# Where the key and value weights begin inside their rows: 64 or 0 bytes past a multiple of 256

## The chip, the core and the metric

The kernel runs on one core of one Trainium2 chip. The metric is the device time of one execution in microseconds (us). Before the change the median of three runs is 750.0 us (749.83 to 750.37).

The core has five engines that run side by side: TensorE (PE in the profile; its loads of stationary operands are listed apart as PEld), VectorE (DVE), ScalarE (ACT), GpSimd (POOL) and SyncE (SP), which here issues the DMAs. A matmul on TensorE has a stationary operand, loaded ahead of it, and a moving operand, streamed past it column by column from SBUF, the core's working memory. Its result lands in PSUM.

## The reference

The kernel mixes two blocks that read the same input x of 2048 tokens by 640 features, with a gate per token:

```python
g = sigmoid((x * gate_w).sum(-1, keepdims=True))
# a: linear attention, 32 heads of 20 features
q, k, v = split(x @ wqkv)
phi_q = concat([softmax(q @ w_phi), softmax(-(q @ w_phi))])   # per head
phi_k = concat([softmax(k @ w_phi), softmax(-(k @ w_phi))])
o = phi_q @ (phi_k.T @ v) / (phi_q @ phi_k.sum(tokens) + 1e-6)
a = o @ wo
# b: feed-forward of width 1728
b = silu(x @ w1) @ w2
return g * a + (1 - g) * b
```

All inputs and the output are float32.

## The kernel before, in words

Every product of float32 matrices is made from two parts of each operand: a high part, which is the value rounded to the matmul's own format, and a low part, the rest. Three products are summed (PASSES: high times high, high times low, low times high), so each matrix product has three passes over the five chunks of 128 input features, fifteen matmuls for one block of output columns.

The work has four stages.

1. **Keys and values.** The key weights are first multiplied with the feature map w_phi (`k_weights`, L332), so that keys come out mapped. Together with the value weights and the gate vector they form 1282 columns. They are kept in two SBUF tiles, `wh` (high parts) and `wl` (low parts), made by `big_kv`. Each holds five rows per partition, one for each chunk of input features, WS = 1344 float32 apart (5376 bytes, 21 times 256). A loop over 16 tiles of 128 tokens then multiplies: the stationary operand is a piece of x (`xa`, 128 by 128), the moving operand is a part of a row of `wh` or `wl`. The first two token tiles are worked while the weights still arrive (`kv_share`, L344), the other fourteen by `kv_proj` (L489). After the products of a tile, `kv_rest` (L470) and `kv_acc` (L459) add the outer products of mapped keys and values of a tile two turns earlier.
2. **Feed-forward**, blocks of 512 tokens: the hidden layer (L537, and L554 for its first four columns of tiles) and the output (L726), both with 512 moving columns.
3. **Queries**, 128 tokens at a time (L448, two halves of 320 columns).
4. **Numerators and output projection**, 256 tokens at a time (L1140 and L1182, 256 columns).

The order on TensorE, VectorE, ScalarE and GpSimd is the order in which the code is written; within the `inorder` blocks it is pinned. All DMAs are issued by SyncE.

The 1282 columns are cut into three parts, one for each PSUM bank: columns 0 to 480, 480 to 980 and 980 to 1282 (CUTS), hence 480, 500 and 302 columns wide. PLACE says at which float32 of a row each part begins: 16, 528 and 1040. The function `w_cols` turns a range of columns into its place in the row, and all who write or read the tiles use it: `k_split_w` and `v_weights`, which write the high part with ScalarE (L125) and the low part with VectorE (L127), and `kv_share` and `kv_proj`, whose matmuls stream it.

The two tiles begin at a multiple of 256 bytes in SBUF and their rows are a multiple of 256 bytes long, so all fifteen parts of a tile begin 64 bytes past a multiple of 256. The pieces of x, the weights and inputs of the feed-forward and of the queries begin at a multiple of 256. The output projection's weights begin 48 float32 (192 bytes) into their tile (WOFF), and the rows it streams at a multiple of 256.

Of the kernel before, what the change touches and what calls it, by code (L numbers as in the profile page):

```python
# [53 lines left out]
WC = 2 * D + 2  # L54
RAW = D + 16
CUTS = (0, 480, 980, WC)
PLACE = (16, 528, 1040)
WS = 1344
VC = PLACE[2] + CUTS[3] - CUTS[2] - (PLACE[1] + D - CUTS[1])
BIG = NC * WS  # L60
# [7 lines left out]
def mix_kernel(ctx: ExitStack, tc: tile.TileContext, xT, wqT, wkc, wkr, wv, bd, bdc, cst, wo, w1, w1r, w2, out):  # L68
# [212 lines left out]
    def part_of(lo, hi):  # L281
        return next(k for k in range(3) if CUTS[k] <= lo and hi <= CUTS[k + 1])

    def w_cols(lo, hi):

        k = part_of(lo, hi)
        return slice(PLACE[k] + lo - CUTS[k], PLACE[k] + hi - CUTS[k])

# [1100 lines left out]
```

## Time and profile before

| | |
|---|---|
| median of 3 runs | 750.0 us (749.83 to 750.37) |
| the profiled execution | 749.77 us |
| its span, first to last instruction | 747.9 us |
| TensorE busy | 742.9 us (99%), 4177 matmuls |
| VectorE, ScalarE, GpSimd busy | 347.5, 264.1, 255.3 us |
| DMA | 50.30 MB, 67 GB/s on average |

The profile is of one execution. It lists groups of instructions by source line (L489 is line 489 of the kernel), engine and operation, with the names of the tile written and of those read, the shape of the operands and a count. A matmul's listed duration reaches from its start to the end of its results, and the next one begins before that: matmuls overlap. What a matmul costs in a dense row of matmuls is the distance from its start to the next start, here called its pitch, which is read from start times in the timeline. Stationary loads (PEld) run beside the matmul before theirs.

### The profile page before, as it was taken

What the parts mean: (1) busy time and instruction counts of PE and PEld (TensorE: products, weight loads), DVE (VectorE), ACT (ScalarE), POOL (GpSimd) and SP (SyncE); (2) the same over time, 40 slices, a digit from 0 to 9 for tenths busy, and PEclk for the clock granted to TensorE, in tenths of its full rate; (3) what the DMA queues carried; (4) which work ended last, traced back from release to release, by engine and by line L of the source; (5) the groups of instructions that cost most, each with busy time, mean ns of one, the idle gap of its engine ahead of it and who ended that gap; (6) DMA issues with size and microseconds to landing.
All of it is one profiled execution on the core that took longest, in us unless ns stands there. A gap on an engine that the chain in (4) does not pass through costs nothing.

```text
span 747.9 us, 10458 instructions
## 1 busy us (share of the span) xinstructions
PE 742.9 (99%) x4177; PEld 648.8 (87%) x4177; DVE 347.5 (46%) x619; ACT 264.1 (35%) x477; POOL 255.3 (34%) x158
## 2 busy tenths in 40 slices
PE   9999999999999999999999999999999999999998
PEld 8899988888888888888888888888898899999988
DVE  5676666676751230112301122032566776867652
ACT  5444443346452321123111221123553534345230
POOL 2488777867200000000000000000174578686540
PEclk9999999999999999999999999999999999999999
DMA  8111111103660130001300013022102221221222
GB/s 264 50 54 53 54 54 53 60 15 103 199 206 1 34 121 1 1 0 40 119 0 1 0 41 122 35 77 65 47 29 99 79 98 58 85 78 57 71 87 78
DMA packets 35304, 50.30 MB, mean 67 GB/s; under 512 B 3546, under 2 KB 22890, under 8 KB 35255
## 3 DMA queue, kind: packets, MB, share of 16 engines
q1 hardware_dynamic: 35255, 49.63, 20.4%
q8 instruction: 33, 0.54, 0.3%
q14 instruction: 16, 0.13, 0.1%
HBM read 38.51 MB, written 11.11 MB: 66 GB/s over the span
## 4 chain that ended last, share of the span: by engine, by line
PE 98%; DMA 1%; SPq 0%; ACT 0%; DVE 0%; issue 0%
PE acc L726 25%; PE ph L537 23%; PE kvp L489 16%; PE pa L1182 10%; PE pq L448 10%; PE pn L1140 3%; PE pT L1007 2%; PE kv L459 2%; PE kvp L554 2%; PE kvp L344 1%; PE kvq L344 1%; PE pwq L239 1%; PE pwk L332 1%; DMA wvr<-wv 1%; PE kvp L470 0%; SPq L190 0%
## 5 line engine op out<-in xcount | busy, mean ns | idle before, releaser
L127 DVE TENSOR_TENSOR u<-ph,u 128x512 fp32r<-128x512 f32 x48 | 33.2, 692 | 186.2 <-ACT u L125 186.2
L726 PE MATMUL acc<-u,w 128*128 128x512 f32 x480 | 113.6, 391 | 0.0
L909 POOL MEMSET kvw<- 120x40 f32 x1 | 0.1, 131 | 309.8 <-PE ph L537 309.8
L726 PEld LDWEIGHTS acc<-u,w 128*128 128x128 f32 x480 | 89.7, 188 | 18.6
L537 PE MATMUL ph<-xf,w 128*128 128x512 f32 x420 | 99.3, 390 | 0.0
L540 ACT ACTIVATE ph<-ph 128x512 f32<-128x512 f32 x48 | 27.9, 582 | 190.4 <-PE ph L537 190.3
L489 PE MATMUL kvp<-wh,xa 128*128 128x480 f32 (+2 forms) x420 | 93.4, 359 | 0.0
L537 PEld LDWEIGHTS ph<-xf,w 128*128 128x128 f32 x420 | 78.7, 188 | 16.2
L489 PEld LDWEIGHTS kvp<-wh,xa 128*128 128x128 f32 x420 | 72.5, 189 | 8.6
L1182 PE MATMUL pa<-oT,wo 128*128 128x256 f32 x600 | 77.0, 282 | 0.0
L1182 PEld LDWEIGHTS pa<-oT,wo 128*128 128x128 f32 x600 | 73.8, 188 | 0.8 <-DVE oT L1161 0.8
L824 POOL TENSOR_TENSOR ez<-eq,zbc 128x1280 f32<-128x1280 f32 x16 | 47.0, 2938 | 79.9 <-ACT eq L807 55.9
L726 PE MATMUL acc<-u,f 128*128 128x512 f32 x300 | 71.6, 391 | 0.0
L537 PE MATMUL ph<-xf,f 128*128 128x512 f32 x300 | 71.3, 390 | 0.0
L537 PEld LDWEIGHTS ph<-xf,f 128*128 128x128 f32 x300 | 56.3, 188 | 11.7
L726 PEld LDWEIGHTS acc<-u,f 128*128 128x128 f32 x300 | 56.1, 188 | 11.5
L127 POOL TENSOR_TENSOR ph<-ek,ph 128x1280 fp32r<-128x1280 f32 x16 | 47.4, 2965 | 27.6 <-ACT ph L125 27.6
L448 PE MATMUL pq<-wq,xb 128*128 128x320 f32 x360 | 55.9, 313 | 0.0
L448 PEld LDWEIGHTS pq<-wq,xb 128*128 128x128 f32 x360 | 52.9, 188 | 2.0 <-DVE oT L1161 1.6
L489 PE MATMUL kvp<-wl,xa 128*128 128x480 f32 (+2 forms) x210 | 47.9, 359 | 0.0
L807 ACT ACTIVATE eq<-eq 128x1280 f32<-128x1280 f32 x16 | 20.4, 1276 | 66.4 <-DVE eq L439 66.4
L489 PEld LDWEIGHTS kvp<-wl,xa 128*128 128x128 f32 x210 | 37.0, 189 | 4.8
(158 smaller groups left out, 1058.9 us busy)
## 6 DMA issues: line engine op xcount, KB each, us to landing
wr<-w SPq DMA_DIRECT2D x26, 320.0 KB, 4.2
xrf<-xT SPq DMA_DIRECT2D x20, 256.0 KB, 3.6
fb_d<-o SPq DMA_DIRECT2D x20, 256.0 KB, 2.4
y<-fb_d SPq DMA_DIRECT2D x16, 256.0 KB, 2.8
out<-y SPq DMA_DIRECT2D x16, 256.0 KB, 2.2
xra<-xT SPq DMA_DIRECT2D x14, 256.0 KB, 3.0
xrb<-xT SPq DMA_DIRECT2D x12, 256.0 KB, 2.7
wvr<-wv SPq DMA_DIRECT2D x5, 327.0 KB, 5.2
```

Source lines behind the costliest of these rows:

```text
L127: eng.tensor_tensor(lo, src, hi.bitcast(F32), op=ALU.subtract)
L344: nc.tensor.matmul(kv_cols(t, lo, hi), x_of(t)[c][:, hx, :], WKV[hw][:, c, w_cols(lo, hi)], start=(opens and hx == 0 and hw == 0), stop=(c ...
L448: nc.tensor.matmul(dst, xt[c][:, hx, :], w[:, c, hw, lo : lo + n], start=first, stop=(hx == 1 and c == NC - 1))
L459: nc.tensor.matmul(kvt[i // 2][: KF + 1, i % 2, :, :KF], vs[t % VB][:, i, : KF + 1], ph[:, :, i * KF : (i + 1) * KF], start=(t == 0 and i ...
L489: nc.tensor.matmul(kv_cols(t, lo, hi), xt[c][:, hx, :], WKV[hw][:, c, w_cols(lo, hi)], start=(n == 0), stop=(n == 3 * NC - 1), skip_group_ ...
L537: nc.tensor.matmul(ph, lhs, rhs, start=(n == 0), stop=(n == len(todo) - 1))
L540: nc.scalar.activation(hs, ph, AF.Silu)
L726: nc.tensor.matmul(acc[m], lhs, rhs, start=(f == order[0] and n == 0), stop=(f == order[-1] and n == len(todo) - 1))
L807: nc.scalar.activation(Q[t]["e"], Q[t]["e"], AF.Exp)
L824: nc.gpsimd.tensor_tensor(ez, Q[t]["e"], zbc, op=ALU.mult)
L1140: nc.tensor.matmul(pns[u, gp][side * CT : side * CT + lhs.shape[-1], a, :], lhs, f[:w, k * 256 : (k + 1) * 256], start=True, stop=True,)
L1182: nc.tensor.matmul(pa[:, a, :], WO[:, c, hw, ds] if c < NG else WOR[:, ds], o[:, ho, c, :] if c < NG else o[:GW, ho, c, :], start=(k == 0) ...
```

## The change

The three parts of each row are moved 16 float32 (64 bytes) towards its beginning, so that they begin at a multiple of 256 bytes. Their widths, the distance between rows, the size of the tiles and the order of all instructions are as they were.

```diff
 CUTS = (0, 480, 980, WC)
-PLACE = (16, 528, 1040)
+PLACE = (0, 512, 1024)
 WS = 1344
 VC = PLACE[2] + CUTS[3] - CUTS[2] - (PLACE[1] + D - CUTS[1])
```

## The prediction

> **What bounds the kernel now.** I read the page's busy shares and its chain first, then TensorE's list of waits, then the groups of matmuls by form, and last the timeline of TensorE, because the question is what one matmul costs from start to next start.
>
> ```profile
> span 747.9 us, 10458 instructions
> PE 742.9 (99%) x4177; PEld 648.8 (87%) x4177; DVE 347.5 (46%) x619; ACT 264.1 (35%) x477; POOL 255.3 (34%) x158
> PEclk9999999999999999999999999999999999999999
> PE 98%; DMA 1%; SPq 0%; ACT 0%; DVE 0%; issue 0%
> PE acc L726 25%; PE ph L537 23%; PE kvp L489 16%; PE pa L1182 10%; PE pq L448 10%; PE pn L1140 3%; PE pT L1007 2%; PE kv L459 2%; PE kvp L554 2%; PE kvp L344 1%; PE kvq L344 1%; PE pwq L239 1%; PE pwk L332 1%; DMA wvr<-wv 1%; PE kvp L470 0%; SPq L190 0%
> ```
>
> ```profile
> PE warm L313 <- DVE ones L166: 1.0, 1, 1.0
> PE kvp L344 <- ACT wh L125: 0.4, 1, 0.4
> PE pT L1007 <- DVE oT L1163: 0.3, 1, 0.3
> ```
>
> TensorE is the whole path: 98% of the chain, at full granted clock in all slices, and idle for 1.7 us in three waits. The change touches the matmuls of lines L489 and L344, which hold 18% of that chain. With nothing waiting in front of them, a nanosecond more or less on each of these matmuls is a nanosecond of the span, so the whole forecast is a count of matmuls times a change in their pitch (start to next start).
>
> **The change, part by part.** No instruction is added, removed or moved in order. The width of the DMA'd value weights, VC, comes out at 654 columns both ways (1040+302-688 and 1024+302-672), so DMA sizes, packets and SyncE's queue stay as they are; the row width WS and the buffers stay too, so no other tile moves. Two things get another address: what ScalarE and VectorE write into the two weight tiles, and what TensorE streams out of them.
>
> The writes:
>
> ```profile
> L125 ACT CAST wh<-pwk x10: 292/425/558, 8.7 to 21.3; 128x480 fp32r<-128x480 f32 x5, 128x160 fp32r<-128x160 f32 x5
> L125 ACT CAST wh<-wvr x6: 439/738/742, 4.3 to 15.8; 128x654 fp32r<-128x654 f32 x4, 128x340 fp32r<-128x340 f32 x1, 128x302 fp32r<-128x302 f32 x1
> ```
>
> These are 16 writes by ScalarE (and 16 alike by VectorE) inside the first 22 us, beside the opening matmuls. What covers them is that TensorE waited for them only once, the 0.4 us above. If another address sped them up, at most that 0.4 us goes; if it slowed them a little, about as much comes. I take 0 and leave 0.4 us each way.
>
> The reads are the whole matter. How many there are:
>
> ```profile
> L489 PE MATMUL kvp<-wh,xa x420: 300/380/416, 32.1 to 172.3; 128*128 128x480 f32 x56, 128*128 128x500 f32 x42, 128*128 128x302 f32 x42
> L489 PE MATMUL kvp<-wl,xa x210: 302/382/396, 33.2 to 171.6; 128*128 128x480 f32 x35, 128*128 128x500 f32 x35, 128*128 128x302 f32 x35
> L344 PE MATMUL kvp<-wh,xa x34: 235/350/492, 5.0 to 24.7; 128*128 128x302 f32 x10, 128*128 128x480 f32 x10, 128*128 128x500 f32 x6, 128*128 128x340 f32 x4
> L344 PE MATMUL kvq<-wh,xa x34: 238/318/426, 5.2 to 32.0; 128*128 128x302 f32 x10, 128*128 128x480 f32 x10, 128*128 128x500 f32 x6, 128*128 128x340 f32 x4
> L344 PE MATMUL kvp<-wl,xa x17: 236/381/425, 5.6 to 24.1; 128*128 128x302 f32 x5, 128*128 128x480 f32 x5, 128*128 128x500 f32 x3, 128*128 128x340 f32 x2
> L344 PE MATMUL kvq<-wl,xa x17: 273/323/396, 5.8 to 31.8; 128*128 128x302 f32 x5, 128*128 128x480 f32 x5, 128*128 128x500 f32 x3, 128*128 128x340 f32 x2
> ```
>
> 420+210+34+34+17+17 = 732 matmuls. L489 runs 14 tokens' tiles times 15 for each of the three parts, 210 each; with L344's 30, 18 and 30 that makes 240 of 480 columns, 228 of 500, 240 of 302; the other 24 are parts of 340 and 160 columns.
>
> What one costs now, from the timeline of one token tile (first number the start in us, the count at the end of the line; a run that goes from the 480s to the 500s is merged, the line of 10):
>
> ```profile
> 102.25 1.26 PE L489 MATMUL kvp<-wh,xa 128*128 128x480 f32 x5
> 103.35 1.26 PE L489 MATMUL kvp<-wl,xa 128*128 128x480 f32 x5
> 104.44 2.40 PE L489 MATMUL kvp<-wh,xa 128*128 128x480 f32 x10
> 106.68 1.30 PE L489 MATMUL kvp<-wl,xa 128*128 128x500 f32 x5
> 107.82 1.30 PE L489 MATMUL kvp<-wh,xa 128*128 128x500 f32 x5
> 108.96 0.49 PE L459 MATMUL kv<-ph,v 128*121 128x240 f32 x3
> 109.29 0.86 PE L489 MATMUL kvp<-wh,xa 128*128 128x302 f32 x5
> 109.99 0.86 PE L489 MATMUL kvp<-wl,xa 128*128 128x302 f32 x5
> 110.69 0.86 PE L489 MATMUL kvp<-wh,xa 128*128 128x302 f32 x5
> 111.39 0.26 PE L470 MATMUL kvp<-ph,v 128*121 128x208 f32 x1
> ```
>
> 480 columns: (104.44-102.25)/10 = 219.0 ns. 500 columns: (108.96-106.68)/10 = 228.0 ns. 302 columns: (111.39-109.29)/15 = 140.0 ns. All three stream rows that begin 64 bytes past a multiple of 256, against stationary tiles (the x tiles) that begin at a multiple of 256.
>
> What matmuls cost whose streamed rows and stationary rows both begin at a multiple of 256, as all of these will after the change:
>
> ```profile
> 536.85 3.56 PE L726 MATMUL acc<-u,w 128*128 128x512 f32 x15
> 540.25 4.56 PE L448 MATMUL pq<-wq,xf 128*128 128x320 f32 x30
> 544.64 3.59 PE L537 MATMUL ph<-xf,w 128*128 128x512 f32 x15
> ```
>
> 512 columns: 3.40/15 = 226.7 ns. 320 columns: 4.39/30 = 146.3 ns. The line through the two is (226.7-146.3)/192 = 0.419 ns a column, and gives 213.3 ns at 480, 221.7 at 500, 138.8 at 302. The key and value matmuls now lie 5.7, 6.3 and 1.2 ns above it. **The end below:** if the shift puts them on the line, 240 x 5.7 + 228 x 6.3 + 240 x 1.2 = 3.1 us are saved.
>
> But two rows speak for the present offset. The output projection is the one other large group whose two operands begin 64 bytes apart modulo 256 (its stationary rows begin at WOFF, 192 bytes, its streamed rows at 0):
>
> ```profile
> 673.63 1.93 PE L1182 MATMUL pa<-oT,wo 128*128 128x256 f32 x15
> 675.40 0.29 PE L1182 MATMUL pa<-oT,wor_s 120*128 120x256 f32 x1
> ```
>
> 1.77/15 = 118.0 ns at 256 columns, where the line gives 119.5: this distance costs 1.5 ns less than none. And line L459 runs ten matmuls a tile in which the streamed rows step by 480 bytes and the stationary rows by 488, so that the distance between the two changes by 8 bytes from one to the next. Stationary rows are read one matmul ahead, so the fourth and the fifth are those that stream while the next weights are read at the same place modulo 256, or 8 bytes off it. Three looks into one tile's ten (ns, least/median/most):
>
> ```profile
> L459 PE MATMUL kv<-ph,v x3: 270/271/273, 58.8 to 59.0; 128*121 128x240 f32 x3
> L459 PE MATMUL kv<-ph,v x2: 271/274/278, 59.3 to 59.4; 128*121 128x240 f32 x2
> L459 PE MATMUL kv<-ph,v x2: 271/272/273, 59.4 to 59.5; 128*121 128x240 f32 x2
> ```
>
> The first look holds matmuls one to three, the second the fifth and sixth, the third the sixth and seventh: the fifth takes 278 ns, the others 270 to 273. So reading the stream and the next weights in step has cost 6 ns here. That the weights are indeed read beside the stream is in the loads' own row, 189 ns each, hidden in the pitches above:
>
> ```profile
> L489 PEld LDWEIGHTS kvp<-wh,xa 128*128 128x128 f32 x420 | 72.5, 189 | 8.6
> ```
>
> **The end above:** 732 x 6 = 4.4 us lost; with the output projection's 1.5 ns it would be 732 x 1.5 = 1.1 us. The change takes away exactly the distance that these rows reward, and the line that speaks the other way is drawn through whole multiples of 64 columns, which 480, 500 and 302 are not. I therefore take the side of the loss, and the mean of its two rows since they are equally near, 3.75 ns: 732 x 3.75 = 2.7 us.
>
> A rule of the Trainium skill stands against that. TensorE: Matmul & The Clock Gate (Part 2, step 1) says that TensorE has two independent read ports of SBUF, and that loading the next weights takes no read bandwidth from the running matmul. By that rule the address could not matter and the sum would be 0; the fifth matmul of L459 does not look like it, though nothing before the change isolates the address.
>
> **Sum.** The profiled execution took 749.77 us for a span of 747.9; with 2.7 us it becomes 750.6 and 752.5. The median of the runs is 750.0, 0.2 above it, so 752.7.
>
> **The rivals.** *First, the excess goes (faster).* The 5.7, 6.3 and 1.2 ns above the line come from streamed rows that begin off a multiple of 256, and vanish: 750.0-3.1 = 746.9 us. For it: 500 columns now cost 228.0 ns and 512 aligned ones 226.7, so something besides length is paid. Against it: 302 columns, at the same offset, pay only 1.2. It decides the sign as soon as the pitches at 480 and 500 fall by more than the 302s rise.
>
> *Second, the address does not matter (no change):* 750.0 us, within the 0.4 us of the writes. For it: the 320-column and 512-column groups cost what they cost with both operands at the same place and no waits, so being in step is harmless there. Against it: the excess at 480 and 500, and L459. This is what the skill's rule on two read ports, named above, would make of it. SBUF — State Buffer (Operand start alignment) asks only for starts at a multiple of the element size and says itself that this is about legality, not speed.
>
> *Third, last blocks are paid whole (slower still).* If an aligned row is read in whole pieces of 256 bytes, 480 and 500 columns cost as much as 512 and 302 as much as 320: 240 x (226.7-219.0) + 228 x (226.7-228.0) + 240 x (146.3-140.0) = 1.8-0.3+1.5 = 3.1 us, and with the 2.7 above 5.8: 755.8 us. For it: the aligned groups in this trace are only whole pieces and cannot deny it. Against it: 480 columns at the present offset also touch eight pieces and are 7.7 ns below 512.
>
> **How the numbers follow.** Forecast (loss of the distance, 752.7) 0.46; third rival 0.14; first 0.28; second 0.12. A measurement of this kernel tells about 0.2%, 1.5 us, from no change: slower is 0.46+0.14 = 0.60, same 0.12, faster 0.28. The range runs from the first rival to the third with the writes' 0.4 us at its ends, 746.8 to 756.2; beyond it I leave the larger losses and gains that no row bounds. The forecast's own range, from 1.5 and 6 ns each, is 751.1 to 754.4.
>
> **What would show it.** In the profile after, the timeline of a token tile: forecast, 480, 500 and 302 columns at about 223, 232 and 144 ns; first rival, 213, 222 and 139; second, 219, 228 and 140; third, 230, 230 and 150. The means of these forms among L489's groups must move by as many nanoseconds, the groups of L726, L537, L448 and L1182 must not move, and the stage of L489 must carry all of the difference. The prediction is wrong if 480 and 500 fall towards the line, or if another stage moves.

## The result, and the profile after

The changed kernel takes 747.93 us (median of 10 runs, 747.34 to 748.16) against 749.9 us before, a ratio of 0.9973 with a 95% interval of 0.9963 to 0.9982. It is 2.0 us faster; the forecast was 2.7 us slower.

The head of the page after, and the row of the L489 matmuls with the high parts (least, median and most duration in ns, then the first and the last start in us):

```profile
span 746.0 us, 10458 instructions
## 1 busy us (share of the span) xinstructions
PE 741.4 (99%) x4177; PEld 648.0 (87%) x4177; DVE 347.3 (47%) x619; ACT 264.1 (35%) x477; POOL 255.3 (34%) x158
```

```profile
L489 PE MATMUL kvp<-wh,xa x420: 297/378/396, 32.1 to 170.4; 128*128 128x480 f32 x56, 128*128 128x500 f32 x42, 128*128 128x302 f32 x42
```

The L489 matmuls start at 32.1 us in both kernels. The last starts at 170.4 in place of 172.3, so the stage is 138.3 us long in place of 140.2, and from there to the end it is 575.6 us both before (747.9-172.3) and after (746.0-170.4). The gain is in the stage of L489. L344's matmuls, which the change touches too, gain 0.1 us: from the second group of L332 (at 10.99 us before and 11.13 after, in the timelines) to the start of L489 it is 21.0 us in place of 21.1. It doesn't show in the start of L489, because the part ahead of them was as much slower in the profiled execution after: its first five matmuls of L344 start 0.2 to 0.5 us apart, where before it was 0.14 to 0.16. The same token tile as in the prediction, from the timeline after:

```profile
101.42 1.24 PE L489 MATMUL kvp<-wh,xa 128*128 128x480 f32 x5
102.50 1.24 PE L489 MATMUL kvp<-wl,xa 128*128 128x480 f32 x5
103.58 2.37 PE L489 MATMUL kvp<-wh,xa 128*128 128x480 f32 x10
105.78 1.28 PE L489 MATMUL kvp<-wl,xa 128*128 128x500 f32 x5
106.90 1.28 PE L489 MATMUL kvp<-wh,xa 128*128 128x500 f32 x5
108.02 0.49 PE L459 MATMUL kv<-ph,v 128*121 128x240 f32 x3
108.35 0.85 PE L489 MATMUL kvp<-wh,xa 128*128 128x302 f32 x5
109.04 0.85 PE L489 MATMUL kvp<-wl,xa 128*128 128x302 f32 x5
109.73 0.85 PE L489 MATMUL kvp<-wh,xa 128*128 128x302 f32 x5
110.42 0.26 PE L470 MATMUL kvp<-ph,v 128*121 128x208 f32 x1
```

480 columns: (103.58-101.42)/10 = 216.0 ns, 219.0 before the change. 500: (108.02-105.78)/10 = 224.0, 228.0 before. 302: (110.42-108.35)/15 = 138.0, 140.0 before. Averaged over all fourteen tiles, from the start times in the trace, the pitches go from 218.6 to 216.7, from 228.7 to 223.7 and from 140.0 to 137.8 ns; 210 x (1.9+5.0+2.2) ns = 1.9 us, which is the stage's gain. The 500-column matmuls carry more than half of it.

### The profile page after: what moved, and what is told of

The parts are those of the page before. It is cut to its first block, busy times and chain, and to the rows that moved or that the text cites. A ratio compares the mean times of both kernels' runs of the same rounds, so it can differ in the third digit from the quotient of the medians.

```text
span 746.0 us, 10458 instructions
## 1 busy us (share of the span) xinstructions
PE 741.4 (99%) x4177; PEld 648.0 (87%) x4177; DVE 347.3 (47%) x619; ACT 264.1 (35%) x477; POOL 255.3 (34%) x158
## 4 chain that ended last, share of the span: by engine, by line
PE 99%; DVE 0%; ACT 0%; issue 0%
PE acc L726 25%; PE ph L537 23%; PE kvp L489 16%; PE pa L1182 10%; PE pq L448 10%; PE pn L1140 3%; PE pT L1007 2%; PE kv L459 2%; PE kvp L554 2%; PE kvp L344 1%; PE kvq L344 1%; PE pwk L332 1%; PE pwq L239 1%; PE warm L313 1%; PE kvp L470 0%; PE pkvt L916 0%
## 5 line engine op out<-in xcount | busy, mean ns | idle before, releaser
L726 PE MATMUL acc<-u,w 128*128 128x512 f32 x480 | 113.6, 390 | 0.0
L726 PEld LDWEIGHTS acc<-u,w 128*128 128x128 f32 x480 | 89.7, 188 | 18.6
L489 PE MATMUL kvp<-wh,xa 128*128 128x480 f32 (+2 forms) x420 | 92.1, 355 | 0.0
L489 PEld LDWEIGHTS kvp<-wh,xa 128*128 128x128 f32 x420 | 71.9, 188 | 8.2
L726 PE MATMUL acc<-u,f 128*128 128x512 f32 x300 | 71.6, 390 | 0.0
L726 PEld LDWEIGHTS acc<-u,f 128*128 128x128 f32 x300 | 56.1, 188 | 11.5
L489 PE MATMUL kvp<-wl,xa 128*128 128x480 f32 (+2 forms) x210 | 47.2, 354 | 0.0
L517 POOL TENSOR_TENSOR ek<-ek,st 128x1280 f32<-128x1280 f32 x16 | 37.9, 2369 | 9.2 <-ACT v L304 6.1
```

The costliest lines, as they stand in the source:

```text
L489: nc.tensor.matmul(kv_cols(t, lo, hi), xt[c][:, hx, :], WKV[hw][:, c, w_cols(lo, hi)], start=(n == 0), stop=(n == 3 * NC - 1), skip_group_ ...
L517: nc.gpsimd.tensor_tensor(groups(e), groups(e), spread(st[:, 1, :]), op=ALU.mult)
L726: nc.tensor.matmul(acc[m], lhs, rhs, start=(f == order[0] and n == 0), stop=(f == order[-1] and n == len(todo) - 1))
```

## The experiments

The first rival had said "faster", because a moving row that starts off a multiple of 256 bytes pays for that. That is one theory; the runs set it beside two others, and the expectations below use their letters.

- **Theory S**: only moving rows that start at a multiple of 256 are cheap.
- **Theory P**: a moving row pays for each piece of 256 bytes that it touches (500 columns touch 9 pieces from a start of 64 and 8 from 0).
- **Theory D**: what counts is the distance, modulo 256, from the start of the stationary rows to that of the moving rows.

"Distance" below is the moving rows' start minus the stationary rows' start, modulo 256 bytes. It was 64 before and is 0 after. Pitches given to a tenth without a row are means over all fourteen tiles (in the other stages, over the whole group), from start times in the trace, without the step into the next group.

### Other starts for the moving rows

Four runs move both weight tiles' rows together. They need a little room, which comes from one output buffer of the feed-forward (here and below, three points stand for lines left out):

```diff
-BIG = NC * WS
+KOFF = 32
+BIG = NC * WS + 64
...
-        return big_tile(name)[:, : NC * WS].rearrange("p (c w) -> p c w", w=WS)
+        return big_tile(name)[:, KOFF : KOFF + NC * WS].rearrange("p (c w) -> p c w", w=WS)
...
-            o = fp.tile([P, 512], F32, tag="o", name=f"o{b}_{m}", bufs=3)
+            o = fp.tile([P, 512], F32, tag="o", name=f"o{b}_{m}", bufs=2)
```

KOFF is 0, 12, 32 or 48 float32, starts of 0, 48, 128 and 192 bytes. The stationary x tiles stay at 0, so the distance equals the start.

> The changed kernel again, with room for the runs beside it: the two weight tiles get 64 more float32 a partition, which leaves every other operand at its place modulo 256, and the feed-forward's output tile o has 2 buffers in place of 3. All theories expect the stage of L489 (first to last start of its matmuls) at 138.3 us as in the changed kernel, with the pitches 216.7, 224 and 138 ns for 480, 500 and 302 columns. The 2 buffers may cost up to 1 us in the feed-forward; if so, the sibling runs are read against this one.

> All moving rows begin 48 bytes past a multiple of 256, the last start (in steps of 16 bytes) at which 500 columns (2000 bytes) still end inside their eighth piece of 256 bytes. Theory P: 500 columns at about 224 ns as at 0, not 228.7 as at 64; 302 and 480 between their values at 0 and 64 (138 to 140 and 217 to 219). Theory S: 219, 229, 140 ns as at 64. Theory D: between the values at 0 and 64 for all lengths, 500 at about 227.

> All moving rows of the key and value weights begin 128 bytes past a multiple of 256. Theory P (a moving row pays for each piece of 256 bytes that it touches): 480 columns touch 8 pieces, as at 0 and 64; 500 touch 9, as at 64; 302 touch 6 in place of 5. So about 217 to 219, 228 and 143 to 145 ns; stage about 140.5 to 141.5 us. Theory S (only a start at a multiple of 256 is cheap): as at 64 bytes, 219, 228, 140 ns; stage 140.2 us. Theory D (the distance between the moving and the stationary rows modulo 256 counts): no number for 128 can be told from 0 and 64, but lengths should move together.

> All moving rows begin 192 bytes past a multiple of 256. Theory P: now 480 columns touch 9 pieces in place of 8, 500 touch 9, 302 touch 6: about 222 to 224, 228 and 143 to 145 ns, the dearest of the four starts, stage about 141.5 to 142.5 us. Theory S: as at 64 bytes, 219, 228, 140 ns, 140.2 us. Theory D: lengths move together.

The same row of each, in the order of starts 0, 48, 128, 192 (the line number is one higher by the edit):

```profile
L490 PE MATMUL kvp<-wh,xa x420: 297/378/396, 31.7 to 169.9; 128*128 128x480 f32 x56, 128*128 128x500 f32 x42, 128*128 128x302 f32 x42
```

```profile
L490 PE MATMUL kvp<-wh,xa x420: 297/376/391, 32.1 to 170.0; 128*128 128x480 f32 x56, 128*128 128x500 f32 x42, 128*128 128x302 f32 x42
```

```profile
L490 PE MATMUL kvp<-wh,xa x420: 299/381/398, 31.8 to 171.5; 128*128 128x480 f32 x56, 128*128 128x500 f32 x42, 128*128 128x302 f32 x42
```

```profile
L490 PE MATMUL kvp<-wh,xa x420: 295/378/411, 32.3 to 169.8; 128*128 128x480 f32 x56, 128*128 128x500 f32 x42, 128*128 128x302 f32 x42
```

The stage takes 138.2, 137.9, 139.7 and 137.5 us. The whole kernel takes 747.90, 747.56, 749.37 and 747.09 us. The first repeats the changed kernel, so the room costs nothing. The last rules out both S and P: at 192 bytes every part touches one piece more than at 0, by P it is the dearest start, and it is the cheapest. Its 500 columns take 221.2 ns, against 223.7 at 0 and 228.7 at 64.

Theory D missed as well in one point: at 48 bytes it had expected every length between its values at 0 and 64. A tile of that run:

```profile
101.18 1.23 PE L490 MATMUL kvp<-wh,xa 128*128 128x480 f32 x5
102.25 1.23 PE L490 MATMUL kvp<-wl,xa 128*128 128x480 f32 x5
103.32 2.35 PE L490 MATMUL kvp<-wh,xa 128*128 128x480 f32 x10
105.51 1.29 PE L490 MATMUL kvp<-wl,xa 128*128 128x500 f32 x5
106.64 1.29 PE L490 MATMUL kvp<-wh,xa 128*128 128x500 f32 x5
107.76 0.49 PE L460 MATMUL kv<-ph,v 128*121 128x240 f32 x3
```

480 columns take (103.32-101.18)/10 = 214.0 ns, 213.6 over all tiles, which is below both 216.7 at 0 and 218.6 at 64; 500 columns take (107.76-105.51)/10 = 225.0. So the lengths do not move together: from 0 to 48 bytes one falls and the other rises, with the same stationary rows.

### The weights moved instead of the stream

Here the stationary x tiles of this stage move, by offset o in a slot with 64 float32 to spare. The room comes from the same output buffer as above, and the line numbers below are three higher:

```diff
-        return (pool or wp).tile([P, 2, 512], F32R, tag=tag, name=name, bufs=bufs)
+        if tag != "x":
+            return (pool or wp).tile([P, 2, 512], F32R, tag=tag, name=name, bufs=bufs)
+        o = 16 if name.startswith("xa") else 0
+        return wp.tile([P, 1088], F32R, tag=tag, name=name, bufs=bufs)[:, o : o + 1024].rearrange("p (a s) -> p a s", a=2)
```

In the first run below the moving rows are at 64 (PLACE as before the change) and the x tiles at 64. In the second the moving rows are at 0 and the x tiles at 64. In the third the moving rows are at 64 and the x tiles at 128 (o = 32). The distances are 0, 192 and 192.

> The moving rows begin at 64 bytes as before the change, and the stationary x tiles of this stage are moved to 64 bytes as well, so that the distance between the two is 0 as in the changed kernel. Theory D: as in the changed kernel, 216.7, 224, 138 ns, stage 138.3 us. Theories S and P (the moving rows' own start): as before the change, 218.6, 228.7, 140 ns, stage 140.2 us.

> The moving rows begin at 0 as in the changed kernel, the stationary x tiles of this stage at 64 bytes, so that the distance is 64 bytes the other way. Theory D: not as in the changed kernel, by 2 ns or more on each length. Theories S and P: as in the changed kernel, 216.7, 224, 138 ns, stage 138.3 us.

> The moving rows of the key and value weights begin at 64 bytes as before the change, the stationary x tiles of that stage at 128, so the moving rows begin 192 bytes past the stationary ones modulo 256, by two starts that no run has had in this pairing. Theory D (the distance counts), with the numbers of the two runs that had a distance of 192 (moving 192 over stationary 0, and moving 0 over stationary 64): stage of L489 at 137.5 us, 137, 217 and 221 ns for 302, 480 and 500 columns. Theory S (the moving rows' own start): as before the change, 140.2 us and 140, 219, 229 ns.

```profile
L492 PE MATMUL kvp<-wh,xa x420: 295/378/396, 32.2 to 171.1; 128*128 128x480 f32 x56, 128*128 128x500 f32 x42, 128*128 128x302 f32 x42
```

```profile
L492 PE MATMUL kvp<-wh,xa x420: 295/377/395, 32.2 to 169.7; 128*128 128x480 f32 x56, 128*128 128x500 f32 x42, 128*128 128x302 f32 x42
```

```profile
L492 PE MATMUL kvp<-wh,xa x420: 295/377/396, 31.9 to 169.4; 128*128 128x480 f32 x56, 128*128 128x500 f32 x42, 128*128 128x302 f32 x42
```

The third is the clearest. Its moving rows start at 64 bytes, exactly as before the change. Only the stationary rows are elsewhere, and the stage falls from 140.2 to 137.5 us. The 500 columns of one of its tiles:

```profile
104.98 1.26 PE L492 MATMUL kvp<-wl,xa 128*128 128x500 f32 x5
106.08 1.27 PE L492 MATMUL kvp<-wh,xa 128*128 128x500 f32 x5
107.19 0.50 PE L462 MATMUL kv<-ph,v 128*121 128x240 f32 x3
```

They take (107.19-104.98)/10 = 221.0 ns. Three runs now have a distance of 192, by three different pairs of starts, and all have a stage of 137.5 us, though single lengths differ by up to 1.2 ns among them. The kernels take 747.09, 746.79 and 747.00 us. In this stage, then, what counts is the distance, and not either start by itself. The second run had been expected to differ from the changed kernel by 2 ns or more at each length; only the 500 columns did (220.3 against 223.7), 480 and 302 stayed within 0.5. The distance is also not quite all: at distance 0 with both at 64 the stage takes 138.9 us, not 138.3, with 500 columns at 226.0 ns in place of 223.7. What the common start adds there is open.

### Shorter rows

Why do 480 and 500 columns stay above the prediction's line (213.3 and 221.7) even at distance 0? Two runs shorten the L489 matmuls of the changed kernel. The columns cut off are left out of the computation, so only pitches are read from these runs (the line numbers are two higher):

```diff
         xt = x_of(t)
+        if 1 < t < NT:
+            hi = lo + min(hi - lo, {480: 448, 500: 496, 302: 288}[hi - lo])
```

The second has 464, 480 and 256.

> The changed kernel, with the matmuls of L489 shortened: 448 columns in place of 480 (seven whole pieces of 256 bytes), 496 in place of 500 and 288 in place of 302; the columns cut off are left out of the computation. The question is why 480 and 500 columns stay above the line through 320 and 512 even when they begin at a multiple of 256. If the length's remainder over whole pieces of 64 columns is what is paid, 448 lies on the line (199.9 ns) and 496 and 288 lie above it by some ns (line: 220.0 and 132.9). If long rows pay whatever their remainder, all of 448 and 496 lie 2 to 4 ns above.

> The changed kernel with 464 columns in place of 480, 480 in place of 500 and 256 in place of 302 in the matmuls of L489; the columns cut off are left out of the computation. By the remainder: 256 on the line (119.5 ns), 464 and 480 above it (line 206.6 and 213.3), and 480 columns in the second part at the 216.7 ns that they take in the first. If instead something about the first two parts' place or their neighbours is paid, 480 in the second part differs from 216.7.

The timeline of a tile in the first, and of one in the second:

```profile
99.72 1.18 PE L491 MATMUL kvp<-wh,xa 128*128 128x448 f32 x5
100.74 1.18 PE L491 MATMUL kvp<-wl,xa 128*128 128x448 f32 x5
101.75 2.29 PE L491 MATMUL kvp<-wh,xa 128*128 128x448 f32 x10
103.89 1.28 PE L491 MATMUL kvp<-wl,xa 128*128 128x496 f32 x5
105.00 1.28 PE L491 MATMUL kvp<-wh,xa 128*128 128x496 f32 x5
106.12 0.60 PE L459 MATMUL kv<-ph,v 128*121 128x240 f32 x4
```

```profile
102.55 1.25 PE L491 MATMUL kvp<-wl,xa 128*128 128x480 f32 x5
103.64 1.24 PE L491 MATMUL kvp<-wh,xa 128*128 128x480 f32 x5
104.72 0.73 PE L459 MATMUL kv<-ph,v 128*121 128x240 f32 x5
105.28 0.76 PE L491 MATMUL kvp<-wh,xa 128*128 128x256 f32 x5
105.88 0.76 PE L491 MATMUL kvp<-wl,xa 128*128 128x256 f32 x5
106.48 0.76 PE L491 MATMUL kvp<-wh,xa 128*128 128x256 f32 x5
107.08 0.26 PE L470 MATMUL kvp<-ph,v 128*121 128x208 f32 x1
```

448 columns take (101.75-99.72)/10 = 203 ns here and 205.2 over all tiles; the line gives 199.9. So a whole number of 64 columns is 5 ns above the line, and the remainder is not what is paid. 496 columns take 223, against 220.0. 480 columns in the second part take (104.72-102.55)/10 = 217.0, as in the first part, so here the place in the row made no difference. 256 columns take (107.08-105.28)/15 = 120.0, on the line. At distance 0, all lengths tried from 448 to 500 lie 2 to 5 ns above a line through 320 and 512. That line is no floor that every length falls to when both operands start at a multiple of 256.

### Does the output projection's row mean what the prediction read in it?

```diff
-WOFF = 48
+WOFF = 0
```

WOFF is 16 in the second run. The moving rows are at 0, so the distance goes from 64 to 0 and to 192.

> The changed kernel with the output projection's stationary rows at 0 in place of 192 bytes (moving rows at 0), a distance of 0 in place of 64. The prediction read the projection's 118.0 ns a matmul (line: 119.5) as a reward for the distance of 64; by that reading its pitch rises to about 119.5 ns, 600 x 1.5 = 0.9 us slower than the changed kernel. Theory D with the key and value matmuls' order of distances (192 cheapest, then 0, then 128 and 64): the pitch falls by 1 to 2 ns, 0.6 to 1.2 us faster.

> The changed kernel with the output projection's stationary rows at 64 in place of 192 bytes, so that the moving rows begin 192 past them. Theory D with the key and value matmuls' order: the cheapest distance, 1 to 3 ns below the present 118.0, 0.6 to 1.8 us faster than the changed kernel. The prediction's reading has no number for it; if the address does not matter for lengths of whole 64 columns, 118.0 stays in this run and in the one with 0.

Fifteen matmuls and the start of the next, of each:

```profile
671.92 1.96 PE L1182 MATMUL pa<-oT,wo 128*128 128x256 f32 x15
673.73 0.28 PE L1182 MATMUL pa<-oT,wor_s 120*128 120x256 f32 x1
```

```profile
671.15 1.88 PE L1182 MATMUL pa<-oT,wo 128*128 128x256 f32 x15
672.86 0.29 PE L1182 MATMUL pa<-oT,wor_s 120*128 120x256 f32 x1
```

1.81/15 = 120.7 ns (119.8 over all) at distance 0, and 1.71/15 = 114.0 (115.0 over all) at 192, against 118.0 at 64. The kernels take 748.90 and 746.33 us, 1.0 slower and 1.6 faster than the changed kernel. So the prediction read this row rightly: at 256 columns a distance of 64 is better than none. It could not be carried to 480, 500 and 302 columns, where 64 is worse than none (at 256 columns in L489, in the second run above, distance 0 gives 119.3, so the level goes with the length and not with the stage).

### The 512-column matmuls

First the feed-forward's moving rows, the x tiles, go to 192 bytes (`o = 48 if name.startswith("xf") else 0` in the slot above, with its room; the line numbers of that run are three higher). Then, with the moving rows left at 0, its stationary tiles f go to 64 and to 192 (16 in the edit below, 48 in the second):

```diff
-                held[k // 5] = big(f"f{k // 5}")
+                held[k // 5] = big(f"f{k // 5}", 16)
```

> The changed kernel with the feed-forward's x tiles at 192 bytes (output tile o with 2 buffers in place of 3, to make room). They are the moving rows of the hidden layer's 512-column matmuls (L537 and L554 before the edit shifts lines; distance 192 in place of 0) and the stationary ones of a quarter of the query matmuls (320 columns, distance 64 in place of 0). Theory D, order of distances as for the key and value matmuls: 512 columns fall below 226.7 ns by 0 to 3, the 320 of that quarter rise above 146.3 by 2 to 6. If only lengths that are no whole multiple of 64 columns feel the distance: 226.7 and 146.3 stay.

> The changed kernel with the stationary tiles f of the feed-forward (300 of the hidden layer's matmuls, 300 of the output's, 512 columns each) at 64 bytes; their moving rows stay at 0, so the distance is 192, as in the run with the x tiles at 192. If it is the distance, these 600 rise from 226.7 to about 233 ns, 4 us slower than the changed kernel in all. If it is the moving rows' start, they stay at 226.7, or fall a little by the order seen at 256, 302 and 500 columns.

> The same stationary tiles f at 192 bytes, a distance of 64. If the order of distances of the key and value stage holds at 512 columns, these 600 rise by 2 to 5 ns; if the start of the moving rows alone counts for whole multiples of 64 columns, they stay at 226.7.

A run of fifteen in the hidden layer and the start of what follows, for moving rows at 192, stationary rows at 64, and stationary rows at 192. In the first, two more rows show the 320-column query matmuls, whose stationary operand is the same x tile:

```profile
288.86 3.66 PE L540 MATMUL ph<-xf,w 128*128 128x512 f32 x15
292.36 3.58 PE L729 MATMUL acc<-u,w 128*128 128x512 f32 x15
...
544.70 4.56 PE L451 MATMUL pq<-wq,xf 128*128 128x320 f32 x30
549.09 1.10 PE L540 MATMUL ph<-xf,w 128*128 128x512 f32 x4
```

```profile
294.32 3.67 PE L537 MATMUL ph<-xf,f 128*128 128x512 f32 x15
297.83 3.57 PE L726 MATMUL acc<-u,w 128*128 128x512 f32 x15
```

```profile
293.81 3.60 PE L537 MATMUL ph<-xf,f 128*128 128x512 f32 x15
297.24 3.56 PE L726 MATMUL acc<-u,w 128*128 128x512 f32 x15
```

3.50/15 = 233.3 ns, 3.51/15 = 234.0 and 3.43/15 = 228.7, against 226.7 in the changed kernel. Over all of the two f groups the means are 233.3 at distance 192, by whichever operand it is made, and 229.1 at 64. The kernels take 754.12, 751.95 and 749.15 us. Here too it is the distance: in the second and third run the streams are untouched. But the order is turned round: by the order of the key and value stage, theory D had expected the first run's 512 columns to fall. Of the distances tried, 0 is the cheapest and 192 the dearest at 512 columns, while 192 is the cheapest at 256 and 500. At 320 columns a distance of 64 costs nothing: 4.39/30 = 146.3, as before, where theory D had expected a rise of 2 to 6.

### Both cheap distances together

Moving rows of keys and values at 0 with their x tiles at 64, and WOFF = 16.

> The changed kernel with both cheap distances: the x tiles of the key and value stage at 64 bytes (moving rows at 0) and the output projection's stationary rows at 64 (moving rows at 0); output tile o with 2 buffers to make room. If the two gains add up: 747.9 - 0.7 (stage of L489 137.5 in place of 138.2) - 1.7 (600 x 2.9 ns) = 745.5 us.

```profile
L492 PE MATMUL kvp<-wh,xa x420: 295/378/396, 31.8 to 169.2; 128*128 128x480 f32 x56, 128*128 128x500 f32 x42, 128*128 128x302 f32 x42
```

The stage is 137.4 us, the projection's pitch 114.9, and the kernel takes 745.04 us, 0.9936 of before (interval 0.9922 to 0.9951). The gains add up, and this version beats both kernels.

## Why the prediction was wrong, point by point

- **TensorE is the whole path, and the sum is a count of matmuls times a pitch: right.** The stage's 1.9 us is the span's 1.9 us, and the later stages keep their 575.6 us to a tenth.
- **The writes by ScalarE and VectorE cost nothing: right within its bounds, as far as the traces can tell.** The L489 matmuls begin at 32.1 us in both kernels, and between 31.7 and 32.4 us in the runs below that have the same starts there.
- **The loss of 3.75 ns a matmul: the step that failed.** It took a price from the output projection (1.5 ns) and from the fifth matmul of L459 (6 ns) and put it on 480, 500 and 302 columns. Measured were gains of 1.9, 5.0 and 2.2 ns. The projection's price was sound: 119.8 ns at distance 0 against 118.0 at 64. What failed was "equally near". The price of a distance depends on the length of the stream, down to its sign: going from 64 to 0 costs 1.8 ns at 256 columns and saves 2.4 at 512 (229.1 to 226.7). The two rows had 256 and 240 columns, the changed matmuls mostly 480 and 500. The 512-column groups, nearest in length, had only one distance in the trace of before and so could give no price.
- **The price read from L459 was unsound as well.** Its three looks left out the fourth, eighth, ninth and tenth of the ten matmuls; the eighth of that same tile takes 277 ns, nearly as much as the fifth (278). And the change moved neither operand of L459, but in the same tile after it the fifth takes 274 ns in place of 278 (its pitch 112 in place of 118), while the eighth still takes 277. So the 6 ns were not the price of that distance alone; what the fifth paid for is open.
- **The first rival (faster, 746.9) had the sign and most of the size, 2.0 of 3.1 us, with a wrong mechanism, so coming close was in part luck.** It had 5.7, 6.3 and 1.2 ns saved at 480, 500 and 302 columns; measured were 1.9, 5.0 and 2.2. Moving rows at 64 are as cheap as any when the stationary rows are at 128 (stage 137.5 us). And 480 columns did not reach the line (216.7 against 213.3), because the line through 320 and 512 is no floor: 448 and 496 columns lie above it too.
- **The second rival (the address does not matter): fallen.** The Trainium skill's TensorE: Matmul & The Clock Gate (Part 2, step 1) has the two SBUF reads independent. Moving nothing but the stationary rows by 64 bytes took the 512-column matmuls from 226.7 to 233.3 ns, so here the measurement decides against reading that sentence as "the place of the weights is free". Its 0.12 was little enough, yet nothing in the trace of before could have excluded it.
- **The third rival (last pieces paid whole): fallen.** It had 480 and 302 columns at 230 and 150 ns, and they took 216.7 and 137.8. At 192 bytes, with one more piece each, 500 and 302 columns fell further.
- **The range and the chances.** The range, 746.8 to 756.2, held the time only because it reached to the first rival. (Its lower end, worked out as it is described, 746.9-0.4, is 746.5.) The 0.60 for slower rested on carrying a price across lengths; with the sign unknown at these lengths it should have been nearer to even.

## What to carry to other kernels

Where TensorE is the path, the starts of both operands' rows modulo 256 bytes are worth a scan, and what to scan is their distance: moving either operand did it here, and the cheaper one to move will do. The two distances chosen in the last run brought this kernel 0.6% in all. Scan for each length of stream by itself, since the best distance tried at 256 and 500 columns (192) was the worst at 512, and 480 columns were cheapest at 48. A price read from a group of another length did not carry over, not even its sign.

## What the runs showed of the hardware that was not expected

- Pitch by distance, in ns (a dash where no run shows it):

| columns | 0 | 48 | 64 | 128 | 192 |
|---|---|---|---|---|---|
| 256 | 119.3 to 119.8 | - | 118.0 | - | 115.0 |
| 302 | 137.8 to 138.3 | 138.1 | 140.0 | 139.8 | 136.9 to 138.0 |
| 320 | 146.5 | - | 146.6 | - | - |
| 480 | 216.7 to 217.7 | 213.6 | 218.6 | 218.9 | 216.2 to 217.4 |
| 500 | 223.7 to 226.0 | 225.0 | 228.7 | 226.7 | 220.3 to 221.2 |
| 512 | 226.7 | - | 229.1 | - | 233.3 |

- 500 columns at distance 192 take 221 ns, 512 at the same distance 233: 12 columns cost 12 ns there, where 0.419 ns a column would give 5.
- Why the distance and the length act together is not settled. The load of the next weights runs during the stream (189 ns each in the prediction's row), and the results fit two reads that disturb each other at certain places, but no run here looks inside a matmul.
- These are means. In the changed kernel the fifteen matmuls of 500 columns take about 222 and 226 ns in turn, although every one of them has the same distance.
- With the x tiles at 192, the output's matmuls (L726, by the edit L729) rose from 226.8 to 228.2 ns though their own operands kept their places modulo 256. The rise sits at the head of each fifteen: the second to the fifth take 229 to 235 ns on average, and from the sixth on all are at 226 to 228. They follow the hidden layer's matmuls at 233, so a matmul's pitch depends also on what ran shortly before it. How is open.
